# Tying the copies of odd value slots to the scores that precede their use, and planning the row transposes with slack

## Chip, cores and metric

One core of one Trainium2 chip runs the whole program. The metric is the time on the device for one execution, in microseconds (us), on that core. The engines work in parallel, each on its own instruction stream in order: TensorE (PE: matmuls, with the weight loads shown apart as PEld), ScalarE (ACT), VectorE (DVE), GpSimd (POOL, here only an issuer of transfers) and SyncE (SP, likewise). They meet only at semaphores.

## The reference

Sliding-window attention over 8 batches, 8 heads, 576 positions and head dimension 64, then a two-layer feed-forward net with a squared ReLU:

```
scores = (1/sqrt(64)) * q @ k^T            # per batch and head
mask   = |pos_q - pos_k| <= 32             # else -1e9
attn   = softmax(scores)
x      = (attn @ v), heads side by side    # 4608 rows x 512
out    = relu(x @ w_in)^2 @ w_out          # 512 -> 2048 -> 512
```

Inputs and output are float32.

## The kernel before

**Chunks and groups.** Each batch is cut into 9 chunks of 64 queries, `c` = 0 to 8; chunk `n = 9*b + c` runs through the kernel's whole life, 72 in all. A chunk needs the 128 keys and values around its 64 queries. Chunks are handled in groups: single chunks and pairs in batches 0 and 1 (in batch 1: chunk 0 alone, then 1-2, 3-4, 5-6, 7-8), and threes from batch 2 on (0-2, 3-5, 6-8). For a group, TensorE computes the scores of all its chunks (`scores`, L570), ScalarE takes the exponential (L583), VectorE multiplies by the band mask, one instruction to a chunk (L590, tile `pt`), TensorE multiplies by the values (`av`, L610 and L611), and VectorE takes reciprocals of the row sums and scales (L627, L629, tile `xr`). The rows are then transposed into `xt`: up to chunk 17 by TensorE and ScalarE (L652, L657), from chunk 18 on by a transposing transfer on SyncE's queue (`xturn`, L640).

**The values.** A load (`vx_load`, L517, issued by POOL) brings values into tile `vx`, five slots of 128 tokens for a batch, two buffers for alternate batches. Even chunks multiply straight from a slot of `vx`. Odd chunks straddle two slots, so VectorE copies the upper half of slot `s` and the lower half of slot `s+1` into slot `s` of tile `vd` (`vd_half`, L529, two copies to a call, `lo` = 0 and 1). Chunk `c` = 2s+1 uses slot `s` of `vd`. From batch 1 on `build` makes two calls per batch, for slots 0-1 and for slots 2-3, beside chunks 1 and 5; a copy then has 64 partitions x 1056 elements. In batch 0 it makes four calls of one slot (64 x 528).

**Queries and keys** are loaded by POOL (L452) and transposed by TensorE in batches 0 and 1 (L475) and by transfers on SyncE's queue from batch 2 on (L510). From batch 2 on every load also waits until TensorE has come to a given block of the feed-forward (`pace`).

**The feed-forward.** Rows come in 9 tiles of 512. `mm1_small`, `mm1_half` and `mm1` (L670, L691, L709) compute `x @ w_in` for a tile into two PSUM buffers `ht`; ScalarE applies ReLU (L676, L697, L715; four buffers `rt`); VectorE squares (L724, tile `gt`); `mm2` (L760) multiplies by `w_out`. These matmuls stand between the attention's steps on TensorE.

**The planner.** No order is written out by hand. Each step is recorded with `rec`: engine, tags that it reads and writes, an assumed duration, a key. Reads of a tag make a step wait for the tag's last writer; the tags become semaphore waits in `emit`. `schedule` then simulates the program with assumed durations and landing times, forward and backward, over three values of padding and three of margin with three rounds each, judges every order found by four simulations with random delays, and keeps the best. That gives each engine one fixed order. A transfer's assumed landing is the end of its simulated service plus a constant, and while an order is searched (`forward` without random delays) also plus its own `slack`:

```
end[op.i] = max(now, start[op.i] + op.dur) + POST[op.eng] + ... + (... if rnd else pad + op.slack)
```

The loads and the transposes of queries and keys from batch 2 on have `slack` = 3000 ns; the row transposes of `xturn` have 0. An order found is judged without slack. A copy of `vd_half` is assumed to take `80 + 145 * (s1 - s0)` ns, so 225 for one slot and 370 for two, and its key is that of the chunk less 3.

Of the kernel before, what the change touches and what calls it, by code (L numbers as in the profile page):

```python
# [21 lines left out]
LEAD = 12  # L22
# [335 lines left out]
class Gen:  # L358
# [161 lines left out]
                   dur=500 + 3.2 * n, move=(n // 2, 13.3, (1000, 900, 800, 800, 800)[s] if b == 0 else 200))  # L520
        self.p.ops[-1].slack = SLACK if b >= FB else 0

    def vd_half(self, b, s0, s1, key):
        vd, vx = self.VD[b % 2], self.VX[b % 2]
        for lo in range(2):
            dst = vd[64 * lo:64 * lo + 64, s0:s1, :, :].rearrange("p s h d -> p (s h d)")
            src = vx[64 - 64 * lo:128 - 64 * lo, s0 + lo:s1 + lo, :, :].rearrange("p s h d -> p (s h d)")
            rd = [("vxl", b % 2, s + lo) + u for s in range(s0, s1) for u in ((), (1,))] + [("vxone", b % 2, k) for k in range(4)]
            self.p.rec("DVE", lambda e, d=dst, c=src: e.tensor_copy(d, c), reads=rd,  # L529
                       writes=[("vd", b % 2, s, lo) for s in range(s0, s1)], key=key, dur=80 + 145 * (s1 - s0), att=True)  # L530

# [21 lines left out]
    def scores(self, n, m):  # L553
        b, c = divmod(n, NCH)
        i = b % 2
        key = n - LEAD
        sc, kt, qt = self.SC, self.KT[i], self.QT[i]
        self.grp += 1
        g = self.grp % 2
        for k in range(m):  # L560
            self.group[n + k] = (self.grp, k, m)

        def f(e):
            for k in range(m):
                for j in range(4):
                    for hm in range(2):
                        r = slice(64 * hm, 64 * hm + 64)
                        o = 512 * hm + (256 * k if k < 2 else 1024)
                        at = 64 * (c + k)
                        mm = e.matmul(sc[:, o + 64 * j:o + 64 * j + 64], kt[r, j, at:at + 128], qt[r, j, at:at + 64],  # L570
                                      start=True, stop=True)
            return mm

        rd = []
        for k in range(m):
            rd += [t for t in self.qk_tags(b, c + k) if t not in rd]
        self.p.rec("PE", f, reads=rd, writes=["sA", "sC"] + (["sB", "sD"] if m > 2 else []),
                   key=key, dur=190 + 115 * m, att=True)
        parts = [("AC", 0, min(m, 2), 0)] + ([("BD", 1024, 1, 1024)] if m > 2 else [])
        for name, o, w, eo in parts:  # L580
            src = bass.AP(sc, o, [[2048, 128], [256, w], [512, 2], [1, 256]])
            dst = bass.AP(self.E[g], eo, [[1536, 128], [512, w], [256, 2], [1, 256]])
            self.p.rec("ACT", lambda e, d=dst, a=src: e.activation(d, a, ACTF.Exp, scale=0.125), reads=["s" + x for x in name],  # L583
                       writes=[("e", g, x) for x in name], key=key, dur=190 + 370 * w, att=True)
        for k in range(m):
            pt = bass.AP(self.PT[(n + k) % 3], 0, [[768, 128], [192, 4], [128, 2], [1, 64]])
            ee = bass.AP(self.E[g], 512 * k, [[1536, 128], [128, 4], [64, 2], [1, 64]])
            mb = bass.AP(self.MASK, 0, [[64, 128], [0, 4], [0, 2], [1, 64]])
            rd = [("e", g, x) for x in ("AC" if k < 2 else "BD")]
            self.p.rec("DVE", lambda e, a=pt, c=ee, d=mb: e.tensor_tensor(a, c, d, ALU.mult),  # L590
                       reads=rd + ["mask"], writes=[("pt", (n + k) % 3)], key=key + k, dur=430, att=True)
# [44 lines left out]
    def xturn(self, n, m, gi):  # L636
        xr = self.XR[gi % 3]
        key = n - LEAD
        if n >= NPE:
            self.p.rec("SP", lambda e: e.dma_start(  # L640
                self.XT[:, n:n + m].rearrange("p n (j h) q -> p (n j) (h q)", j=2), xr[:, 0:m].rearrange("p n x -> p (n x)"),
                transpose=True), reads=[("xr", gi % 3, u) for u in range(m)], writes=[("xt", n + u) for u in range(m)],
                dma=(f"x{gi % 3}", n), key=key, dur=1250, move=(16 * m, 28), att=True)
            return

        trp, tag = (self.TRP, "sD") if n >= 8 else (self.OUTP[0][:].bitcast(BF16), ("outp", 0))

        def f(e):
            for u in range(m):
                for t in range(2):  # L650
                    o = 256 * u + 128 * t
                    mm = e.transpose(trp[:, o:o + 128], xr[:, u, 128 * t:128 * t + 128], self.ID)  # L652
            return mm

        self.p.rec("PE", f, reads=[("xr", gi % 3, u) for u in range(m)] + ["id"], writes=[tag], key=key, dur=112 * m, att=True)
        src = trp[:, 0:256 * m].rearrange("p (n f q) -> p n f q", n=m, f=4)
        self.p.rec("ACT", lambda e: e.activation(self.XT[:, n:n + m], src, ACTF.Copy),  # L657
                   reads=[tag], writes=[("xt", n + u) for u in range(m)], key=key, dur=200 + 180 * m, att=True)
# [132 lines left out]
    def build(self):  # L791
# [18 lines left out]
        for b in range(B_):  # L810
            while 8 * tile + 7 < NCH * b:
                self.moe(tile)
                tile += 1
            if b < FB:
                if not b:
                    self.first_load("k", "SP", -300)
                    self.first_load("q", "ACT", -300)
                for bb in range(0 if b else FB):
                    for x in range(6):
                        for t in "kqv":  # L820
                            if f"{t}{bb}{x}" not in at:
                                continue
                            if t == "v":
                                self.vx_load(bb, x, at[f"v{bb}{x}"])
                            else:
                                self.tok_load(bb, t, x, at[f"{t}{bb}{x}"])
            else:
                for x in range(5):
                    kb = 9 * b - 40 + 2 * x
                    for t in "kq":  # L830
                        self.tok_load(b, t, x, kb)
                        self.dma_turn(b, t, x, 9 * b - LEAD - 9 + 2 * x)
                    self.vx_load(b, x, kb + 0.1)
            for c in range(NCH):
                n = NCH * b + c
                m = 3 if b >= FB else 1 if not c or n in (1, 8) else 2
                if n not in self.group:
                    if n == 0:
                        self.tok_turn(0, 0, -LEAD - 3)
                    if n == 8:  # L840
                        self.moe(0)
                        tile = 1
                        self.tok_turn(0, 5, -LEAD + 5)
                    self.scores(n, m)
                    if b < FB and n + m < FB * NCH:
                        bb, cc = divmod(n + m, NCH)
                        if n + m != 8:
                            self.tok_turn(bb, (cc + 1) // 2 if bb else TURN0[cc], n + m - LEAD - 3)
                if c and not b:
                    x = (c + 1) // 2  # L850
                    if c % 2:
                        self.vd_half(b, x - 1, x, n - LEAD - 3)
                if b and c in (1, 5):
                    self.vd_half(b, c // 2, c // 2 + 2, n - LEAD - 3)
                self.av(n)
                gi, k, m = self.group[n]
                if n < 2:
                    self.evac(n, 1, 0, n)
                    if n:
                        self.xturn(0, 2, 0)  # L860
                elif k == m - 1:
                    self.evac(n - k, m, gi, 0)
                    self.xturn(n - k, m, gi)
# [41 lines left out]
```

## Time and profile before

| | us |
|---|---|
| median of 13 runs (310.52 to 313.27) | 312.0 |
| the profiled execution | 313.09 |
| its span, first to last instruction | 311.3 |
| busy: PE / PEld / DVE / ACT / POOL | 299.3 / 169.9 / 142.3 / 149.2 / 106.9 |

| costliest groups | count | busy us | mean ns |
|---|---|---|---|
| L760 second-layer matmuls, 128x512 | 528 | 132.6 | 381 |
| L709 first-layer matmuls, 128x512 | 448 | 113.3 | 379 |
| L715 ReLU on ScalarE | 112 | 66.7 | 599 |
| L724 square on VectorE | 144 | 60.8 | 424 |
| L590 mask on VectorE | 72 | 27.3 | 421 |
| L529 copies into `vd` | 36 | 18.1 | 503 |

Busy times add up the durations of single instructions merged in time; the records of pipelined matmuls overlap, so that a matmul's start after the one before it says more of the rate than its duration. Lines such as L529 are lines of the kernel before. "Granted clock" is the share of full speed that TensorE's clock gate allowed. A "releaser" is the instruction or transfer whose semaphore ended an engine's idle time. The time outside the span is 313.09 - 311.3 = 1.8 us.

### The profile page before, as it was taken

The page shows a single profiled execution, that of the slowest core. Times are in us where ns is not written, and L with a number is a line of the kernel's source. Part 1 is how long each engine was busy: PE and PEld are TensorE (multiplying, and loading weights), DVE is VectorE, ACT ScalarE, POOL GpSimd, SP SyncE. Part 2 cuts the span into 40 slices and gives each one's busy share as a digit, 9 for nine tenths or more (in the row PEclk, how much of TensorE's full clock was granted, in tenths as well). Part 3 has the DMA queues.
Part 4 walks back from the last instruction along what each step waited for, and adds up shares of the span by engine and source line. Part 5 has one row for each costly group of instructions (what it writes and reads, how often), then busy time and mean ns, then how long its engine had stood idle before and what let it go on. Part 6 is the DMA issues. An engine that isn't in the chain of part 4 may idle for free.

```text
span 311.3 us, 7009 instructions
## 1 busy us (share of the span) xinstructions
PE 299.3 (96%) x2843; PEld 169.9 (55%) x2843; DVE 142.3 (46%) x361; ACT 149.2 (48%) x243; POOL 106.9 (34%) x133
## 2 busy tenths in 40 slices
PE   8778999969999999999999999999999999999996
PEld 7567845866755545455445445444445444444444
DVE  6765434645556655555355345444445332222200
ACT  3366523534656665555545545554545543434411
POOL 8999292232414554333333343343330000000000
PEclk9799999998999999999999999999999999999999
DMA  9999999999999999999999999999994220000012
GB/s 110 154 190 206 187 172 175 193 136 177 86 142 141 128 139 161 187 123 150 162 148 99 156 132 141 131 106 138 179 144 65 61 61 34 34 34 36 34 76 93
DMA packets 166096, 39.06 MB, mean 125 GB/s; under 512 B 157232, under 2 KB 161584, under 8 KB 166064
## 3 DMA queue, kind: packets, MB, share of 16 engines
q0 software_dynamic: 115200, 18.16, 85.0%
q1 hardware_dynamic: 44896, 10.95, 25.0%
q10 hardware_dynamic: 5968, 9.51, 9.5%
q8 instruction: 22, 0.36, 0.5%
q14 instruction: 10, 0.08, 0.1%
HBM read 36.70 MB, written 9.44 MB: 148 GB/s over the span
## 4 chain that ended last, share of the span: by engine, by line
PE 85%; DMA 8%; DVE 3%; POOL 1%; issue 0%; ACT 0%; POOLq 0%; DVEq 0%
PE outp L760 34%; PE ht L709 31%; DMA vx<-in_v_dram 8%; PE ht L670 5%; PE sc L570 3%; PE sc L610 3%; PE sc L611 3%; PE sc L760 2%; PE ht L691 2%; DVE vd L529 1%; DVE xr L629 1%; PE sc L734 1%; PE outp L734 1%; PE outp L652 1%; POOL vx L517 1%
## 5 line engine op out<-in xcount | busy, mean ns | idle before, releaser
L760 PE MATMUL outp<-w,gt 128*128 128x512 bf16 x528 | 132.6, 381 | 0.0
L709 PE MATMUL ht<-xt,w 128*128 128x512 bf16 x448 | 113.3, 379 | 0.0
L715 ACT ACTIVATE rt<-ht 128x512 bf16<-128x512 f32 x112 | 66.7, 599 | 84.4 <-PE ht L709 81.5
L724 DVE TENSOR_TENSOR gt<-rt 128x512 bf16<-128x512 bf16 x144 | 60.8, 424 | 100.0 <-ACT rt L715 87.0
L760 PEld LDWEIGHTS outp<-w,gt 128*128 128x128 bf16 x528 | 49.9, 98 | 56.2 <-issue 0.6
L709 PEld LDWEIGHTS ht<-xt,w 128*128 128x128 bf16 x448 | 41.6, 98 | 46.6 <-issue 0.2
L452 POOL DMA_DIRECT2D qraw<-in_q_dram x40 | 35.3, 883 | 47.2 <-PE ht L709 31.9
L452 POOL DMA_DIRECT2D kraw<-in_k_dram x40 | 35.2, 881 | 45.3 <-PE ht L709 18.6
L517 POOL DMA_DIRECT2D vx<-in_v_dram x40 | 35.4, 888 | 32.5 <-PE ht L709 9.3
L583 ACT ACTIVATE e<-sc 128x1024 bf16<-128x1024 f32 (+1 forms) x47 | 37.3, 823 | 14.4 <-PE sc L570 14.4
L590 DVE TENSOR_TENSOR pt<-e,mask 128x512 bf16<-128x512 bf16 x72 | 27.3, 421 | 22.5 <-ACT e L583 22.4
L767 ACT ACTIVATE oe<-outp 128x512 f32<-128x512 f32 x33 | 19.8, 598 | 22.1 <-PE outp L760 22.1
L670 PE MATMUL ht<-xt,w 128*128 128x128 bf16 x384 | 24.3, 223 | 0.8 <-ACT xt L657 0.7
L629 DVE TENSOR_TENSOR xr<-sc,rs 128x768 bf16<-128x768 f32 (+2 forms) x29 | 23.7, 818 | 1.2
L529 DVE COPY vd<-vx 64x1056 bf16<-64x1056 bf16 (+1 forms) x36 | 18.1, 503 | 13.4 <-DMA vx<-in_v_dram 12.4
L670 PEld LDWEIGHTS ht<-xt,w 128*128 128x128 bf16 x384 | 22.6, 100 | 1.6 <-ACT xt L657 0.9
L676 ACT ACTIVATE rt<-ht 128x512 bf16<-128x512 f32 x24 | 14.2, 599 | 16.5 <-PE ht L670 16.5
L610 PE MATMUL sc<-vx,pt 128*128 128x65 bf16 x160 | 15.2, 193 | 1.3 <-DVE pt L590 1.3
L570 PEld LDWEIGHTS sc<-qt,kt 64*128 64x128 bf16 x576 | 10.2, 96 | 9.6 <-issue 5.3
L611 PE MATMUL sc<-vx,pt 128*128 128x65 bf16 x160 | 15.2, 195 | 0.0
L610 PE MATMUL sc<-vd,pt 128*128 128x65 bf16 x128 | 12.2, 194 | 2.4 <-DVE pt L590 2.4
L610 PEld LDWEIGHTS sc<-vx,pt 128*128 128x128 bf16 x160 | 12.1, 98 | 4.1 <-DVE pt L590 1.9
(64 smaller groups left out, 162.2 us busy)
## 6 DMA issues: line engine op xcount, KB each, us to landing
out_dram<-oe ACTq DMA_DIRECT2D x35, 256.0 KB, 3.3
kraw<-in_k_dram POOLq DMA_DIRECT2D x30, 128.0 KB, 5.3
qraw<-in_q_dram POOLq DMA_DIRECT2D x30, 128.0 KB, 5.6
vx<-in_v_dram POOLq DMA_DIRECT2D x24, 128.0 KB, 5.2
w<-in_moe_w_in_dram POOLq DMA_DIRECT2D x4, 512.0 KB, 10.2
w<-in_moe_w_out_dram POOLq DMA_DIRECT2D x4, 512.0 KB, 17.9
vx<-in_v_dram POOLq DMA_DIRECT2D x16, 96.0 KB, 5.6
kt<-kraw SPq DMA_TRANSPOSE x30, 5.2
```

The source lines that it names most:

```text
L452: self.p.rec("POOL", lambda e: e.dma_start(dst, src), writes=[("fraw", b, t, x)], old=[("fraw", b - 2, t, y + (b == 2))], reads=self.pace( ...
L517: self.p.rec("POOL", lambda e: e.dma_start(self.VX[b % 2][r:r + n, s, :, 0:64], self.v[b, :, t0:t0 + n, :].rearrange("h p d -> p h d")), w ...
L583: self.p.rec("ACT", lambda e, d=dst, a=src: e.activation(d, a, ACTF.Exp, scale=0.125), reads=["s" + x for x in name], writes=[("e", g, x) ...
L590: self.p.rec("DVE", lambda e, a=pt, c=ee, d=mb: e.tensor_tensor(a, c, d, ALU.mult), reads=rd + ["mask"], writes=[("pt", (n + k) % 3)], key ...
L610: e.matmul(o, pt[:, a:a + 128], vt[:, ha, 0:VE], start=True, stop=False)
L611: mm = e.matmul(o, pt[:, a + 64:a + 192], vt[:, ha + 2, 0:VE], start=False, stop=True)
L629: self.p.rec("DVE", lambda e: e.tensor_tensor(bass.AP(xr, 256 * k, [[768, 128], [256, m], [64, 4], [1, 64]]), bass.AP(self.SC, base, [[204 ...
L670: mm = e.matmul(ht[:, 128 * (d % 4):128 * (d % 4) + 128], self.W1[:, ft, 128 * d:128 * d + 128], self.XT[:, t0 // 64:t0 // 64 + 2, ft, :], ...
L709: mm = e.matmul(ht[:], self.W1[:, ft, 128 * d:128 * d + 128], self.XT[:, 8 * T:8 * T + 8, ft, :], start=(ft == 0), stop=(ft == 3))
L715: self.p.rec("ACT", lambda e: e.activation(rt[:], ht[:], ACTF.Relu), reads=[("ht", k % 2)], writes=[("rt", k % 4)], key=key, dur=560)
L724: self.p.rec("DVE", lambda e: e.tensor_tensor(g, r, r, ALU.mult), reads=[("rt", k % 4)], writes=tags, key=key, dur=430)
L760: mm = e.matmul(op, gt[:, d, 128 * u:128 * u + 128], self.W2[:, d, :], start=(d == 0), stop=(d == 15))
```

## The change

Three edits. `scores` now also writes a tag `("sc", n)`, n being the group's first chunk. `vd_half` takes extra tags to read (`tie`), and from batch 1 on it is called once for each group, for the slots of the group's odd chunks alone, with that group's tag, so that a copy waits for the scores of the group that uses it; its key is the chunk's own, no longer 3 less. The slots and so the shapes change with it: in batch 1 four calls of one slot; from batch 2 on one slot for chunk 1, two slots for chunks 3 and 5, one slot for chunk 7. Batch 0 stays as it was. The row transposes on SyncE's queue get a `slack` of 1500 ns, which enters the planner's search and no instruction.

```diff
-    def vd_half(self, b, s0, s1, key):
+    def vd_half(self, b, s0, s1, key, tie=()):
...
-            rd = [("vxl", b % 2, s + lo) + u for s in range(s0, s1) for u in ((), (1,))] + [("vxone", b % 2, k) for k in range(4)]
+            rd = list(tie) + [("vxl", b % 2, s + lo) + u for s in range(s0, s1) for u in ((), (1,))] + [("vxone", b % 2, k) for k in range(4)]
...
-        self.p.rec("PE", f, reads=rd, writes=["sA", "sC"] + (["sB", "sD"] if m > 2 else []),
+        self.p.rec("PE", f, reads=rd, writes=["sA", "sC"] + (["sB", "sD"] if m > 2 else []) + [("sc", n)],
                    key=key, dur=190 + 115 * m, att=True)
...
                 dma=(f"x{gi % 3}", n), key=key, dur=1250, move=(16 * m, 28), att=True)
+            self.p.ops[-1].slack = 1500
             return
...
-                if b and c in (1, 5):
-                    self.vd_half(b, c // 2, c // 2 + 2, n - LEAD - 3)
+                if b and not self.group[n][1]:
+                    odd = [c + u for u in range(self.group[n][2]) if (c + u) % 2]
+                    if odd:
+                        self.vd_half(b, odd[0] // 2, odd[-1] // 2 + 1, n - LEAD, [("sc", n)])
                 self.av(n)
```

## The prediction

> **What bounds the kernel.** I read the page first, then TensorE's waits, then stretches of time around each wait, then VectorE's order of work there.
>
> ```profile
> PE 299.3 (96%) x2843; PEld 169.9 (55%) x2843; DVE 142.3 (46%) x361; ACT 149.2 (48%) x243; POOL 106.9 (34%) x133
> PE   8778999969999999999999999999999999999996
> PEclk9799999998999999999999999999999999999999
> ```
>
> TensorE is busy nearly always; every other engine has half its time free. So time can come only from slices (7.8 us each) where PE's digit, or the clock's, is below 9: the first four, and one place more, the ninth and tenth (62 to 78 us). TensorE's own waits, and the one of VectorE that matters:
>
> ```profile
> PE sc L610 <- DVE pt L590: 3.8, 3, 2.4
> PE outp L652 <- DVE kt L491: 2.3, 2, 1.3
> DVE vd L529 <- DMA vx<-in_v_dram: 12.4, 7, 4.1
> ```
>
> The columns are total, times, longest. The longest wait of TensorE, 2.4 us, is for a mask on VectorE, an engine with half its time free: something holds the mask up. Stretches of time (width; busy PE, PEld, DVE, ACT, POOL; clock; DMA share; GB/s):
>
> ```profile
> 49.00:51.00 2.00, 1.49 (x20) 0.90 (x18) 1.61 (x5) 0.00 (x0) 0.20 (x1) 1.00 1.89 233
> 62.00:65.70 3.70, 3.70 (x77) 3.51 (x75) 0.43 (x1) 2.51 (x5) 1.52 (x2) 1.00 1.27 109
> 65.70:68.25 2.55, 0.19 (x5) 0.04 (x1) 1.16 (x4) 0.48 (x1) 1.02 (x2) 1.00 1.84 160
> 68.25:72.40 4.15, 4.06 (x36) 2.85 (x36) 3.28 (x10) 0.60 (x1) 0.88 (x1) 0.59 2.43 158
> 72.40:300.00 227.60, 227.60 (x1878) 115.24 (x1878) 101.78 (x235) 115.59 (x188) 59.78 (x71) 1.00 1.07 113
> ```
>
> After 72.4 us TensorE never pauses and has the full clock: nothing can be gained there, only lost. The losses that a change from batch 1 on can reach lie between 49 and 72.4 us. VectorE's order there:
>
> ```profile
> 61.52 0.41 DVE L724 TENSOR_TENSOR gt<-rt 128x512 bf16<-128x512 bf16 x1
> 64.25 0.43 DVE L529 COPY vd<-vx 64x1056 bf16<-64x1056 bf16 x1 [2.31 <-DMA vx<-in_v_dram]
> 67.06 0.43 DVE L529 COPY vd<-vx 64x1056 bf16<-64x1056 bf16 x1 [2.38 <-DMA vx<-in_v_dram]
> 67.52 0.43 DVE L724 TENSOR_TENSOR gt<-rt 128x512 bf16<-128x512 bf16 x1
> 67.86 0.75 DVE L590 TENSOR_TENSOR pt<-e,mask 128x512 bf16<-128x512 bf16 x2
> ```
>
> Two copies for batch 2 (slots 0-1) stand ahead of the masks of batch 1's chunks 14 and 15, and wait 4.7 us for loads. The second of these, by the chain of waits, was 21 us under way behind other loads:
>
> ```profile
> 45.92 21.12 DMA vx<-in_v_dram
> ```
>
> Scores of chunks 14-15 end at 63.43, their exponential at 64.70; TensorE runs out of other work at 65.9 and gets the masks only at 68.3. The values that held it up are first used by batch 2, whose scores start at 79.87.
>
> **Part one, the tie.** A copy can no longer stand ahead of the scores of its own group, so no copy of batch 2 comes before about 75 us, 8 us after the last of these landings (67.04). *The wait of 2.45 us at 65.9 goes.* Without the copies the two masks would run from about 64.7 to 65.5, before TensorE is free. *The clock:* in the row 68.25 to 72.4 it is 0.59, so 4.15 x 0.41 = 1.70 us of TensorE's time is lost, with the matrix unit busy throughout (sixteen L670 matmuls take 1.90 us there, 1.06 at 62.03). That half-speed stretch follows the gap; the two gaps for L652 above (1.0 and 1.3 us, at 17 and 23 us) and the 0.5 us at 49.4 had none behind them. So it goes too: 1.70. *The 49 us stretch:* a copy for slots 2-3 waits 1.50 us there ahead of the mask of chunk 9; TensorE loses 2.00 - 1.49 = 0.51. With the copy behind the scores of chunks 14-15 (63 us) this goes: 0.51. Sum of gains 2.45 + 1.70 + 0.51 = 4.66.
>
> The Trainium skill, "TensorE: Matmul & The Clock Gate", Part 1, has the clock fall after at least one idle window of about 3.4 us; by that a gap of 2.5 us should not cost the clock, and the gain would be 2.96. The trace differs, its 2.45 us gap was followed at once by half clock, and I go by the trace.
>
> **Part two, the copies themselves.**
>
> ```profile
> L529 DVE COPY vd<-vx 64x1056 bf16<-64x1056 bf16 x28 | 13.1, 468 | 11.9 <-DMA vx<-in_v_dram 11.1
> L529 DVE COPY vd<-vx 64x528 bf16<-64x528 bf16 x8 | 5.0, 625 | 1.6 <-DMA vx<-in_v_dram 1.4
> ```
>
> 28 double copies become 12 double and 32 single (batch 1: 8 single; batches 2 to 7: 4 single and 2 double each). A double one takes 0.43 in a calm stretch. For a single one outside the start no row exists: below, half a double one, 0.22; above, the mean of the eight of this shape at the start, 0.63, among the heaviest loads. I take 0.36, the fastest of those eight, since later stretches are calmer. VectorE: 32 x 0.36 + 12 x 0.43 - 13.1 = +3.6 us (ends -0.9 and +12.3), on an engine with 169 free: 146 of 311 busy. Hidden under TensorE unless it comes between a group's scores and its products.
>
> The Trainium skill, "VectorE: DVE Perf Modes", section on the TRN2 errata, speaks against this edit: each instruction from SBUF pays a fixed cost, so a copy should be cut into few large pieces. With the page's measured fixed 150 cycles an estimate for a single copy is (150 + 132)/0.96 = 294 ns, and VectorE's sum would be +1.5 us; the double copy by that estimate, 431 ns, is what the trace has.
>
> That place is now just where they stand. One steady group, TensorE then VectorE:
>
> ```profile
> 86.38 0.53 PE L570 MATMUL sc<-qt,kt 64*128 64x64 bf16 x24
> 86.83 2.76 PE L760 MATMUL outp<-w,gt 128*128 128x512 bf16 x12
> 89.43 0.19 PE L610 MATMUL sc<-vd,pt 128*128 128x65 bf16 x1
> ```
>
> ```profile
> 86.95 0.43 DVE L529 COPY vd<-vx 64x1056 bf16<-64x1056 bf16 x1
> 87.41 0.42 DVE L724 TENSOR_TENSOR gt<-rt 128x512 bf16<-128x512 bf16 x1
> 88.03 1.10 DVE L590 TENSOR_TENSOR pt<-e,mask 128x512 bf16<-128x512 bf16 x3 [0.19 <-ACT e L583]
> ```
>
> Between the end of scores (86.90) and the first mask (88.03) lie 1.13 us in which ScalarE works on the exponential; here a copy and a square fit into them. Over all groups from chunk 10 on, but for 14, the gap is 1.10 to 1.39 us, with at most one square (0.43) in it in all but this group. Two single copies (0.72) and a square make 1.15, late by 0.05; two double ones and a square 1.29, late by 0.2. TensorE comes to a chunk's product 0.8 to 1.0 us after its mask in nearly every group (at 89.43 against 88.45), held there by its matmuls. Three groups have less: chunk 27 (0.12 and 0.06), chunk 16 (0.37), chunk 30's second (0.31). I charge 0.1 each for two of them, +0.2 (0 to 0.8, where single copies take 0.63).
>
> **What queues behind the new wait.** Behind a tied copy on VectorE stand squares and masks; ScalarE's four `rt` buffers and TensorE wait for squares. The masks wait for the same scores by way of the exponential, at least 1.1 us longer, so the tie adds no later wait to that queue, only an earlier one. The loads that refill a `vx` slot wait for its copy: slot 1 is now read until the group of chunk 3 (about 87 us in batch 2), and batch 4's loads begin after 100 us: nothing.
>
> **Part three, the slack.** It issues nothing: 18 row transposes and 60 of keys and queries stay on SyncE's queue, at 1.2 us each, about 95 of 311 us. It only lets the search put first-layer matmuls later behind other work. Today none waits for `xt` after 72.4, so its gain is 0; it can cost where TensorE lacks other work. Bounds: -0.3 (the L670 waits for `xt`, 0.7 in all, lie earlier and mostly stay) and +1.5 once. I take 0.
>
> **Sum.** 313.09 - 4.66 + 0.2 = 308.6 for the profiled execution, which stands 1.1 above the median: 312.0 - 4.46 = **307.5**.
>
> **Rivals.**
> *A, forecast, 307.5, chance 0.67.* Own range 306.0 to 309.5: half clock may fall differently from run to run (1.7), and the start shifts a little.
> *B, the late loads are still the bound, 309.7, chance 0.07.* TensorE now runs 4.7 us ahead while loads land as before. For it: 21 us in flight. Against: the last late piece of batch 2, its fourth block of queries, is transposed at 68.25 and needed at about 82. Half the gain returned: 312 - 2.3.
> *C, the copies land in the path, 314.5, slower, chance 0.16.* If the planner, which assumes 225 ns for a single copy, puts each pair behind the group's masks, the odd product waits. With 0.72 or 0.86 for a pair, TensorE comes 0.54 after the last mask for a middle chunk (short by 0.18) and 0.27 for a first one (short by 0.59): a batch of three groups loses 0.18 + 0.59 + 0.18, six batches 5.7; batch 1's four pairs, 0.34 after the last mask, 4 x 0.38 = 1.5. Together 7.2 against 4.66. It decides from 0.21 us a group over 22 groups. Against: the planner knows both chains, and the gap ahead of the masks is free.
> *D, nothing in sum, 312.0, chance 0.10.* The order is searched anew for the whole program; the first 40 us hold 40 - 33.5 = 6.5 us without matmul, which another order can widen as well as narrow. Against: keys and loads of batch 0 are unchanged. That the tie fails to do what it says is excluded by the dependence; only where the time goes is open.
>
> **Chances.** About 0.3% (0.9 us) is what a measurement of this kernel can tell from no change. Faster: 0.65 of A, 0.06 of B, 0.03 of D = 0.74. Slower: 0.15 of C and 0.03 of D = 0.18. The rest, 0.08, same. The range goes from 305.6 (A's low end less 0.4 for the start) to 311.8, which leaves out C and half of D.
>
> **What would show it.** Right: no `vd` copy waits for a load after 45 us; TensorE's wait for masks falls from 3.8 us to under 1; no half clock between 60 and 80 us; single copies near 0.36. Wrong: a gap of over 1.5 us anywhere after 45 us, a new group of waits of TensorE for L529, or first-40-us gaps above 8 us.

## The result, and the profile after

The changed kernel takes 308.93 us in the median (307.50 to 310.80, 11 runs) beside 312.01 for the kernel before (48 runs): ratio 0.9894, 95% interval 0.9869 to 0.9920. It is faster, by 3.1 us; forecast were 4.5. Its profiled execution took 308.44 us with a span of 306.6, 4.7 less than before. From its page, and TensorE's waits (total, times, longest):

```profile
PE 296.5 (97%) x2843; PEld 167.6 (55%) x2843; DVE 143.6 (47%) x377; ACT 148.5 (48%) x243; POOL 106.8 (35%) x133
PE   8588999999999999999999999999999999999996
PEclk9999999999999999999999999999999999999999
```

```profile
PE ht L671 <- DMA w<-in_moe_w_in_dram: 1.7, 1, 1.7
PE outp L653 <- DVE kt L491: 1.4, 2, 0.8
```

The ninth and tenth slices are full now, of work and of clock. The 3.8 us of waits for masks (L610 on L590) are gone from the list; what is left lies in the first 26 us. Line numbers after L640 are one higher than before. VectorE's waits:

```profile
DVE vd L529 <- PE sc L570: 14.6, 22, 1.5
DVE pt L590 <- ACT e L583: 8.0, 14, 1.7
DVE vd L529 <- DMA vx<-in_v_dram: 1.7, 3, 1.2
```

The copies' waits for loads fell from 12.4 to 1.7 us, all of it in batch 0. In their place 22 copies wait for scores, 14.6 us together: idle time that VectorE used to spend a little later, waiting for the exponential (L590 on L583: 22.4 before, 8.0 now). VectorE around the place of the old gap:

```profile
63.01 1.00 DVE L529 COPY vd<-vx 64x528 bf16<-64x528 bf16 x2 [1.54 <-PE sc L570]
64.05 0.42 DVE L725 TENSOR_TENSOR gt<-rt 128x512 bf16<-128x512 bf16 x1
64.39 0.75 DVE L590 TENSOR_TENSOR pt<-e,mask 128x512 bf16<-128x512 bf16 x2
```

The copies that stand here now are those of chunk 14 itself (the odd chunk of the pair 14-15), for values long there, and the masks begin at 64.39 where they began at 67.86. Starts of scores in both profiles say where the time came from:

| stretch, from scores to scores | before | after | difference |
|---|---|---|---|
| span's start to chunk 8 | 44.11 | 44.34 | +0.23 |
| chunk 8 to chunk 10 | 7.91 | 7.22 | -0.69 |
| chunk 10 to chunk 14 | 11.00 | 11.00 | 0.00 |
| chunk 14 to chunk 16 | 9.40 | 5.04 | -4.36 |
| chunk 16 to the end | 238.9 | 239.0 | +0.1 |

Two places hold it all, the two that the prediction named. In sum nothing was won or lost in the 239 us behind them.

### The profile page after: what moved, and what is told of

Same layout as the page of the kernel before. It is cut to its first block, busy times and chain, and to the rows that moved or that the text cites. A ratio compares the mean times of both kernels' runs of the same rounds, so it can differ in the third digit from the quotient of the medians.

```text
span 306.6 us, 7029 instructions
## 1 busy us (share of the span) xinstructions
PE 296.5 (97%) x2843; PEld 167.6 (55%) x2843; DVE 143.6 (47%) x377; ACT 148.5 (48%) x243; POOL 106.8 (35%) x133
## 4 chain that ended last, share of the span: by engine, by line
PE 92%; DMA 3%; POOL 2%; DVE 1%; ACT 0%; issue 0%; POOLq 0%
PE outp L761 37%; PE ht L710 32%; PE ht L671 7%; PE sc L570 3%; PE sc L610 3%; PE sc L611 3%; DMA w<-in_moe_w_in_dram 3%; PE ht L692 2%; PE sc L761 2%; POOL vx L517 1%; PE sc L475 1%; PE sc L735 1%; PE outp L735 1%; POOL kraw L452 1%; POOL qraw L452 1%; PE sc L653 1%
## 5 line engine op out<-in xcount | busy, mean ns | idle before, releaser
L725 DVE TENSOR_TENSOR gt<-rt 128x512 bf16<-128x512 bf16 x144 | 60.7, 424 | 95.1 <-ACT rt L716 85.1
L583 ACT ACTIVATE e<-sc 128x1024 bf16<-128x1024 f32 (+1 forms) x47 | 37.3, 823 | 10.1 <-PE sc L570 10.1
L590 DVE TENSOR_TENSOR pt<-e,mask 128x512 bf16<-128x512 bf16 x72 | 27.2, 420 | 8.1 <-ACT e L583 8.0
L529 DVE COPY vd<-vx 64x528 bf16<-64x528 bf16 (+1 forms) x52 | 19.9, 382 | 17.2 <-PE sc L570 14.6
L671 PE MATMUL ht<-xt,w 128*128 128x128 bf16 x384 | 23.6, 219 | 2.4 <-DMA w<-in_moe_w_in_dram 1.7
L610 PE MATMUL sc<-vx,pt 128*128 128x65 bf16 x160 | 15.0, 192 | 0.1
L627 DVE RECIPROCAL rs<-sc 128x12 f32<-128x12 f32 (+2 forms) x29 | 6.3, 218 | 16.1 <-PE sc L611 15.8
L570 PE MATMUL sc<-qt,kt 64*128 64x64 bf16 x576 | 13.5, 191 | 0.3 <-ACT qt L488 0.2
```

Of the source, the lines that this page charges most:

```text
L610: e.matmul(o, pt[:, a:a + 128], vt[:, ha, 0:VE], start=True, stop=False)
L671: mm = e.matmul(ht[:, 128 * (d % 4):128 * (d % 4) + 128], self.W1[:, ft, 128 * d:128 * d + 128], self.XT[:, t0 // 64:t0 // 64 + 2, ft, :], ...
L725: self.p.rec("DVE", lambda e: e.tensor_tensor(g, r, r, ALU.mult), reads=[("rt", k % 4)], writes=tags, key=key, dur=430)
```

## The experiments

The first row repeats the result above. The others were timed beside the kernel before in three sessions, in which that kernel's median was 311.25, 311.61 and 312.16 us; so ratios are compared, not times. A ratio here is the record's own, with its interval; it differs from the quotient of the two medians by up to 0.002 (0.6 us).

| kernel | median us | ratio to before | 95% interval |
|---|---|---|---|
| the change | 308.93 | 0.9894 | 0.9869 to 0.9920 |
| the change, again | 308.04 | 0.9901 | 0.9872 to 0.9931 |
| three copies moved by hand | 309.43 | 0.9951 | 0.9925 to 0.9977 |
| gap filled with matmuls | 311.81 | 1.0002 | 0.9979 to 1.0024 |
| tie without slack | 309.24 | 0.9917 | 0.9890 to 0.9945 |
| slack alone | 312.61 | 1.0036 | 1.0006 to 1.0066 |
| split without tie | 313.14 | 1.0034 | 1.0008 to 1.0061 |
| tie without split | 308.68 | 0.9903 | 0.9877 to 0.9928 |
| copies made twice | 309.70 | 0.9938 | 0.9918 to 0.9958 |
| matmuls in the start | 308.70 | 0.9904 | 0.9871 to 0.9937 |
| weights one place earlier | 308.32 | 0.9900 | 0.9864 to 0.9936 |

**Three copies moved, nothing else.** The planner's order of the kernel before is kept; after planning, VectorE's list is changed in one place.

```diff
         p.schedule()
+        late = [o for o in p.ops if getattr(o, "name", None) in (("vd", 2, 0, 0), ("vd", 2, 0, 1), ("vd", 2, 2, 0))]
+        rest = [o for o in p.ops if o not in late]
+        at = [getattr(o, "name", None) for o in rest].index(("vd", 2, 2, 1))
+        p.ops = rest[:at] + late + rest[at:]
```

> The order of the kernel before, with three copies of batch 2 (slots 0-1, both halves, and the first half of slots 2-3) moved on VectorE alone, to behind the masks of chunks 16 and 17. Theory (the gain is the copies' place ahead of the masks of chunks 14-15): the 2.45 us gap near 66 us goes, and with it the half clock; what is left of the change is the 0.5 us at chunk 9. The span falls by 2.4 to 4.2 us against the kernel before. Rival (the gain is a new order of the whole program): within 0.9 us of the kernel before, the wait turns up at another place.

The span fell by 3.9 us, to 307.4; from the scores of chunk 14 to those of chunk 16 it takes 5.04 us, as in the change. So the place of these copies is the cause of the gap, with every other instruction where it was. By the ratio the gain is only about half of the change's (0.9951 beside 0.9894); by medians of one session it comes closer (309.43 us beside 309.24 for the tie without slack, below), so how far it falls short is not settled. Its profile shows two losses that the change does not have. A copy still waits ahead of chunk 9's mask, as in the kernel before: chunk 8 to chunk 10 takes 7.82 us, and 7.22 in the change. The other stands a few us behind the old gap, on VectorE:

```profile
69.91 1.35 DVE L529 COPY vd<-vx 64x1056 bf16<-64x1056 bf16 x3
72.47 0.43 DVE L529 COPY vd<-vx 64x1056 bf16<-64x1056 bf16 x1 [1.21 <-DMA vx<-in_v_dram]
72.93 0.21 DVE L628 RECIPROCAL rs<-sc 128x8 f32<-128x8 f32 x1
73.17 0.69 DVE L630 TENSOR_TENSOR xr<-sc,rs 128x512 bf16<-128x512 f32 x1
```

TensorE is 4.4 us ahead now, and the fourth copy of batch 2, which waited for nothing in the kernel before, meets its load 1.21 us too early, ahead of the scaling of chunks 16 and 17. TensorE then waits 0.75 us to transpose those rows. A place fixed by hand moves the wait; the tie, which ties the copy to its use, does not have this one.

**The gap filled.** Again the order of the kernel before, with 40 matmuls on zeros put ahead of the products of chunk 14, into the bank that those products overwrite.

```diff
         p.schedule()
+        at = [getattr(o, "name", None) for o in p.ops].index(("av", 14))
...
+        w.deps = {d for d in av.deps if getattr(d, "name", None) != ("pt", 14)}
+        w.fn = lambda e: [e.matmul(bank[:, 0:128], self.ZZ[:, 0:128], self.ZZ[:, 0:128], start=True, stop=True)
+                          for _ in range(40)][-1]
+        p.ops = p.ops[:at] + [w] + p.ops[at:]
```

> The order of the kernel before, with 40 matmuls on zeros (2.2 us at full clock) on TensorE ahead of the products of chunk 14, so that the gap near 66 us stays but TensorE is not idle in it. Theory (the half clock comes from the gap): no half clock from 68 to 73 us; the masks' wait stays, so 1.7 us of the 4.15 come back in the profile, and less than that in the median if the half clock falls in part of the executions only. Rival (the clock falls on its own schedule, or the gap alone counts): half clock as before, time within 0.5 us of the kernel before, or slower.

Two stretches of its profile (width; busy PE, PEld, DVE, ACT, POOL; clock; DMA share; GB/s):

```profile
66.10:68.40 2.30, 2.30 (x47) 2.30 (x44) 1.79 (x6) 0.47 (x1) 1.26 (x2) 1.00 2.20 165
68.40:72.00 3.60, 3.55 (x61) 2.54 (x60) 2.56 (x8) 1.47 (x2) 0.88 (x1) 1.00 2.61 146
```

The clock stays at 1.00 behind the filled gap (0.59 in the first profile), and chunk 14 to 16 takes 7.27 us where it took 9.40: the profile agrees with the theory. The median does not gain: in time the rival was right. Worked out as below, the clock takes at most 0.6 us of an execution on average, against 1.4 in the kernel before in the same session, so something else costs about as much. That the 2.2 us of matmuls overrun the gap where it is short would fit (7.27 us here beside 6.79 in the third profile of the kernel before, below, where the gap was short and the clock stayed full), and was not shown.

**The parts of the change, one at a time.**

```diff
 # tie without slack: the change less this line
-            self.p.ops[-1].slack = 1500
 # slack alone: the kernel before and this line
+            self.p.ops[-1].slack = 1500
 # split without tie: the change, but
-                        self.vd_half(b, odd[0] // 2, odd[-1] // 2 + 1, n - LEAD, [("sc", n)])
+                        self.vd_half(b, odd[0] // 2, odd[-1] // 2 + 1, n - LEAD)
 # tie without split: the change, but with the calls of before
+                if b and c in (1, 5):
+                    self.vd_half(b, c // 2, c // 2 + 2, n - LEAD, [("sc", n - self.group[n][1])])
```

> The change without the slack of the row transposes. Theory (the tie is all of the gain): 3 us faster than the kernel before, as the change, within 0.7 us of it. Rival (the slack has a share): over 0.9 us slower than the change, with a wait of TensorE for rows after 80 us.

> The kernel before with the slack of the row transposes and nothing else. Theory (slack is worth nothing here): within 0.9 us of the kernel before, the wait for masks near 66 us still there, unless the new search happens to move the copies. Rival: 1 us or more faster with the wait still there.

> The change without the tie: one call of copies to a group, with the chunk's own key, free to stand anywhere. Theory (the tie does it): the search puts copies early again, VectorE waits for value loads between 40 and 70 us as before (over 8 us in all, against 1.7 in the change), and the time is within 1 us of the kernel before. Rival (smaller copies for the group alone do it, as each waits for two slots only and not for three): at least 1.5 us faster than the kernel before, VectorE's wait for loads under 4 us.

> The calls of the kernel before (slots 0-1 and 2-3, double copies) with the tie to the scores of the group that needs them first, and the slack. Theory: as the change within 0.9 us, since only the place of the copies counts and VectorE is half idle either way; VectorE's wait for loads under 3 us. Rival (the tie without the split makes a group wait for a slot that it does not need): slower than the change by over 0.9 us, with TensorE waiting for L529 or for masks.

Both kernels with the tie are as fast as the change as far as can be told (0.9917 and 0.9903; the intervals overlap). Both without it are no faster than the kernel before, a little slower if anything (1.0036 and 1.0034): that is 1.1 us each, just outside the 0.9 and 1 us expected, and the cause was not looked for. A small share of the slack is not excluded: without it the ratio is 0.0023 higher, 0.7 us, and the profile has a wait of TensorE, at 150 us, that neither profile of the change has:

```profile
PE sc L570 <- DMA qt<-qraw: 1.1, 1, 1.1
```

That is a wait for transposed queries, in one execution. The split without the tie shows why the smaller copies alone do nothing: the planner puts them early again.

```profile
PE sc L610 <- DVE pt L590: 3.3, 3, 2.5
DVE vd L529 <- DMA vx<-in_v_dram: 11.1, 6, 5.2
```

The waits of before are all there, 2.5 us of TensorE for a mask, 11.1 of VectorE for values. The tie without the split:

```profile
DVE vd L529 <- PE sc L570: 8.7, 13, 1.6
DVE vd L529 <- DMA vx<-in_v_dram: 2.2, 3, 1.3
```

So of the three edits the tie is what acts. The copies' new key, which came with it, is in the split without tie as well, and did nothing there.

**Copies made twice.** Is there really room for them between scores and masks? Ahead of each copy from batch 1 on the same copy goes into a tile that nothing reads.

```diff
         p.schedule()
+        ops, last = [], {}
+        for o in p.ops:
+            m = getattr(o, "name", None)
+            if m and m[1] > 0:
...
+                w.deps = set(o.deps) | ({last[lo]} if lo in last else set())
+                w.fn = lambda e, m=m: e.tensor_copy(m[2], m[3])
+                last[lo] = w
+                ops.append(w)
+            ops.append(o)
+        p.ops = ops
```

> The order of the change, and ahead of each copy from batch 1 on the same copy once more into a tile that nothing reads: 44 copies more, 32 x 0.294 + 12 x 0.43 = 14.6 us of VectorE between scores and masks. Theory (there is cover: 1.1 us of free time ahead of the masks and 0.8 to 1.0 us between a mask and TensorE's use): the masks come 0.2 to 1.0 us later, TensorE waits in few groups, 0 to 2 us in all slower than the change. Rival (the copies are in the path): 0.3 to 0.6 us a group, 7 to 14 us slower than the change.

The added copies, and all that TensorE waited for masks:

```profile
L882 DVE COPY xd<-vx 64x528 bf16<-64x528 bf16 x32 | 10.0, 311 | 11.3 <-PE sc L572 10.8
L882 DVE COPY xd<-vx 64x1056 bf16<-64x1056 bf16 x12 | 5.6, 469 | 3.8 <-PE sc L572 3.6
```

```profile
PE sc L612 <- DVE pt L592: 0.5, 1, 0.5
```

15.6 us more work on VectorE, at the place where it could hurt most, cost (0.9938 - 0.9901) x 311.6 = 1.2 us, and one wait of 0.5 us, at chunk 27, one of the groups that the prediction named as short of room. The two intervals overlap, so the 1.2 is known to about 1 us; the profile has a like size, 240.1 us from chunk 16 to the end where the change has 239.0. The change itself has only the first of the two sets of copies there, and in its second profile, as in its first, TensorE waits for no mask and no copy after 45 us: its copies are covered.

**Two more profiles of the kernel before.**

> The kernel before, a second profile. Theory (the first profile was an execution with more lost time than most: 313.09 against a median of 312.0): the gap ahead of the products of chunk 14 is there again, 1.2 to 2.5 us, since the copies ahead of the masks wait for the same load; a half-clock stretch of 3.4 us behind it in some executions only, so that the place between the scores of chunks 14 and 16 takes 7.5 to 9.4 us (9.4 in the first profile, 5.0 in the changed kernel). Rival: no gap or one under 1 us, so that the first profile misled.

> The same as the look before it, a third profile of the kernel before: gap ahead of the products of chunk 14 of 1.2 to 2.5 us, half clock behind it or not.

These executions took 312.8 and 311.19 us. TensorE's wait for the masks in the one, then in the other:

```profile
PE sc L610 <- DVE pt L590: 1.9, 1, 1.9
```

```profile
PE sc L610 <- DVE pt L590: 1.5, 1, 1.5
```

And the stretch behind it, in the one, then in the other (columns as above):

```profile
68.10:72.00 3.90, 3.89 (x52) 2.36 (x52) 3.06 (x9) 0.60 (x1) 0.88 (x1) 0.69 2.94 118
```

```profile
67.80:71.00 3.20, 3.20 (x57) 2.34 (x58) 2.99 (x9) 0.93 (x2) 0.88 (x1) 1.00 3.53 111
```

The wait is always there and never the same: 2.4, 1.9, 1.5 us. The half clock followed it in two of the three. Chunk 14 to 16 took 9.40, 8.21 and 6.79 us; the last is below the range expected. The other place varies as well: chunk 8 to chunk 10 took 7.91, 7.23 and 7.31 us, beside 7.22 in the change, so that the 0.7 us gained there by the first profile are 0.1 or less by the others. The profile that the prediction was made from was the unluckiest of the three.

**Two tries for more.** Both start from the change. In one, 24 matmuls on zeros go ahead of the first first-layer step, where TensorE waits 1.7 us for weights; in the other that load is issued one place earlier.

```diff
 # one
+        p.ops = p.ops[:at] + fill + p.ops[at:]
 # other
-ORDER = ("k01 q01 v00 v01 k02 q02 v02 w10 k03 q03 v03 w11 k04 q04 v04 w12 w13 w20 w21 w22 w23 k05 q05 "
+ORDER = ("k01 q01 v00 v01 k02 q02 w10 v02 k03 q03 v03 w11 k04 q04 v04 w12 w13 w20 w21 w22 w23 k05 q05 "
```

> The changed kernel's order, with 24 matmuls on zeros (1.3 us at full clock) ahead of the first first-layer step at 14 us, where TensorE waits 1.7 us for weights in the profile of the changed kernel. Theory (what still sets the changed kernel's runs apart is a half-clock stretch in the start, in 5 of 12 runs, 1.6 us each): fewer such runs, median 0 to 0.8 us lower than the change, never below 307. Rival (the matmuls delay TensorE where the weights are there): the same or up to 1 us slower.

> The change, with the first piece of the first-layer weights loaded one place earlier, ahead of the third piece of values. Theory (TensorE's longest wait left is the 1.7 us for this load): that wait falls under 0.9 us, the copies of slot 1 in batch 0 wait for values instead for up to 0.9 us; 0 to 0.9 us faster than the change. Rival (the start is bound by the loads as a whole): same as the change within 0.9 us, the wait only moves.

The wait fell, to 0.2 and to 0.4 us, and the time did not (0.9904 and 0.9900, the change has 0.9894 and 0.9901). The time to the scores of chunk 8 hardly moved, 44.14 and 43.37 us where the two profiles of the change have 44.34 and 43.75. That the loads of the start bind as a whole, the rival for the second, fits this and was not shown. Four of the first kernel's twelve executions took 311.4 to 313.3 us, and none of 18 of the change over 310.8. Its profile is of one of the four, 312.85 us, so it says nothing of the median; it does show a wait that the change comes close to:

```profile
86.16 1.19 SPq L510 DMA_TRANSPOSE kt<-kraw  x1
87.39 1.42 SPq L640 DMA_TRANSPOSE xt<-xr  x1
```

```profile
93.99 1.02 PE L711 MATMUL ht<-xt,w 128*128 128x512 bf16 x4 [3.07 <-DMA xt<-xr]
```

The rows of chunks 21 to 23 were scaled by 85.72, but their transpose stood on SyncE's queue behind one for keys, which itself waited for its load; issued at 87.39 it landed 6.5 us later, and TensorE, 4.8 us earlier at this place than in the kernel before, stood still for 3.07 us and then had half clock from 95.1 to 98.5. In the change's own profile the same transpose is issued at 85.94 and nothing waits; the rows land there at 90.18, 0.8 us before their first use. Whether the other three had the same wait is not known.

## Why the prediction was right, and by how much it was off

**What bounds, and where the gain is: right.** Two places, chunk 9 and chunks 14-15, and nothing after 72.4 us. The table of stretches has -0.69 and -4.36 there against -0.51 and -4.15 forecast, for the execution that was read. Moving three copies by hand shows that their place alone makes the gap.

**Its size in the median: too large.** Forecast 4.46, measured 3.08. The mis-sized terms are all three gains, read from one execution and taken for all. In the three profiles of the kernel before, set against the change's, the two places hold 5.05, 3.18 and 1.84 us, 3.4 on average, which is near what was measured. *The gap, 2.45:* 2.4, 1.9 and 1.5 us. *The clock, 1.70:* a half-clock stretch followed in two of the three. *The 49 us stretch, 0.51:* 0.7, 0.0 and 0.1 us. What the clock's term is worth on average stays open. Each timed execution comes with its mean granted clock, and (1 - clock) x span is the most that it can have cost. For the 68 of the kernel before that were timed beside the experiments this is 1.45 us on average, for the 18 of the change 0.82: 0.6 less, give or take as much. But among executions with the full clock alone (25 and 11) the change is 3.2 us faster (311.16 and 307.98 on average), as much as over all of them, which would leave the clock nothing. The execution that was read was an unlucky one, and the forecast took its losses for the rule. Since the clock falls in some executions only, such a term belongs in the sum with its share of the executions; a second profile would have shown it.

**The clock's rule.** The Trainium skill, "TensorE: Matmul & The Clock Gate", Part 1, gives a free-running window of 3413 ns and half rate after an idle window of about 3.4 us. The traces agree with the window: within a profile all changes of the granted clock lie on one grid of 3.413 us (the stretches that begin at 10.72 and 68.74 us in the first profile are 17 steps apart, those at 14.98 and 69.60 in the second 16), each half-clock stretch that ends inside a span lasts one step, and the grid lies elsewhere in each execution. They do not agree with the threshold: the gaps of 2.4 and 1.9 us were followed by half clock, and by the page's threshold none should have been; the trace decides. Summed step by step, in the twelve profiles whose clock records fix the grid, TensorE was idle for 1.65 to 2.51 us of the 3.41 in each of the thirteen steps inside a span that half clock followed, and for at most 1.71 us in each of the 1062 others. As an estimate from these numbers, about half a step of idle time is enough, in one gap or in several (1.89 us in pieces ahead of 10.72 us). The prediction's gaps at 17 and 23 us (at most 1.27 us in a step) and the 1.5 us of the third profile fall short of that; the filled gap leaves no idle time in its steps and had full clock behind it. By this estimate a gap of 2 us costs the clock only where the grid leaves most of it in one step.

**The cost of the copies: right in kind, too high in size.** A single copy takes 0.294 us in calm stretches (the median of all; the mean in the row below, 352 ns, takes in the eight of the start), where 0.36 was taken for the later ones; VectorE is busy 143.6 us, not 146. (The upper end of that sum comes to +12.2, not +12.3.)

```profile
L529 DVE COPY vd<-vx 64x528 bf16<-64x528 bf16 x40 | 14.1, 352 | 13.2 <-PE sc L570 10.8 <-DMA vx<-in_v_dram 1.7
```

The Trainium skill, "VectorE: DVE Perf Modes", section on the TRN2 errata, warned of the fixed cost of small copies; an estimate from its 150 cycles was 294 ns, and that is the duration measured. The warning holds for the copy and not for the kernel, where that work is covered. The 0.2 us charged to short groups stands: the products of chunk 27 start at 94.36 us, 0.1 behind the end of their mask, and by the spacing of the matmuls before them 0.25 late. That is the one loss that appeared after 72 us.

**The new wait, and the refills: right.** 22 copies wait for scores and no TensorE wait follows. **The slack: right to count as nothing, as far as can be told;** alone it brought nothing, and the tie without it brings all but 0.7 us by the ratios, within the noise. **The signs of being wrong** did not show: no gap over 1.5 us after 45 us, no wait of TensorE for copies, 7.5 us without matmul in the first 40.

**The rivals.** Copies in the path (314.5) is refuted by doubling them: 1.2 us for twice the work. Nothing in sum (312.0) is refuted by the ratio. Late loads as the next bound (309.7) has something to it: TensorE running ahead met a late load in the hand-made order (0.75 us) and a late transpose once (3.07 us), and in the change's profile such a transpose is only 0.8 us ahead of its use. In the median of the change there is no sign of it that was measured apart.

## What to carry to other kernels

An instruction that can be made early may be put early by a planner that works with assumed landing times, as in all three orders searched here without the tie, and on an engine that works in order it then holds up work that has nothing to do with it. Tie such a step to the event that announces its use; where the engine has idle time just there, the tie is free. Read a stall's size from more than one profile before summing it, above all what the clock adds behind it.

## What the runs showed of the hardware that was not expected

The clock's loss is a matter of chance in the same program, as a grid that lies elsewhere in each execution would have it: of 68 timed executions of the kernel before 25 had a mean clock of 0.999 or 1.000, 31 of 0.994 or 0.995 (one stretch of 3.413 us at half rate is 0.5 x 3.413 / 311 = 0.55%), 12 of 0.988 or 0.989 (two). Executions with two were no slower on average than those with one (311.99 and 312.06 us; 311.16 with none); that some stretches fall where TensorE waits anyway would fit, and was not shown. And eight of the 40 loads of values, issued between 20 and 49 us, took 19 to 21 us from issue to landing in the first profile, while the median of the larger kind, 128 KB, is 5.2.
